# First pair's loads and rotation regrouped, and a new hand-placed order of the attention steps

## The chip, the cores and the metric

The kernel runs on one NeuronCore of a Trainium2 chip. The metric is the device time of one execution in microseconds (us). The engines are named as in the profile: PE is TensorE (matrix products and transposes), PEld its weight loads, DVE is VectorE, ACT is ScalarE, POOL is GpSimd, and SP is SyncE, whose queue (SPq) issues nearly all transfers.

## What is computed

The reference takes q, k and v of shape (2 batches, 8 heads, 576 positions, 64 columns), rotates q and k by the rotary tables, and computes softmax attention. Its output, 1152 tokens of 512 columns, goes through an RMS norm and a gated MLP (width 1536), and then through four expert MLPs whose outputs are weighted by the normalised domain probabilities. All is float32.

```python
def rotate(x):
    x1, x2 = (x[..., :half], x[..., half:])
    return np.concatenate([x1 * cos - x2 * sin, x1 * sin + x2 * cos], axis=-1)
q_rot, k_rot = (rotate(q), rotate(k))
scores = scale * np.matmul(q_rot, k_rot.transpose(0, 1, 3, 2))
attn = np.exp(scores - np.max(scores, axis=-1, keepdims=True))
attn = attn / (np.sum(attn, axis=-1, keepdims=True) + 1e-09)
return np.matmul(attn, v).astype(np.float32)
```

## The kernel before

Attention goes over eight pairs of heads (four pairs for each batch), `attention_pair` at L1096. Of a head's 576 positions the first 512 are "main": partition p holds positions 4p to 4p+3, so that a pair's main part is eight columns of 64 (j = 0 to 3 for the first head, 4 to 7 for the second). The last 64 positions of both heads share a ninth column, j = 8, the "left" rows. `rotate` (L551) does four steps with the tables -sin, sin and cos: two products into a scratch tile, a product in place, and a sum that lands in `turned`, tile by tile of 128 positions. `turn` (L604) transposes ten 64x64 pieces on PE into PSUM, copies the result into KQ (q scaled), and `dup` (L623) copies KQ's halves to the other partitions (KQ2) with two transfers on SP, since a head's scores need its keys and queries on both halves. For q such a copy has 144 KB, for k 72 KB.

For each pair there are nine tiles of scores, `s_step` (L650): matrix products into two PSUM banks, the row maximum on DVE (L680), the exponential on ACT (L684). `t_tile` transposes the exponentials and copies them to PTX; `pv` multiplies them with v; `scale` turns the reciprocal sums. Pair 0's first two tiles use own halves only and write both heads with one group (L664). When batch 0 is through, `rms_mean` (DVE, then twelve tiny operations on POOL from L848 on) and `rms_spread` prepare the norm.

Beside attention the first weights are prepared. SP loads 512 KB into a raw buffer (`w_load`, L363); ACT and DVE join and split it (`w_first`, `w_low`, `w_join`, `w_parts`), and `w_rest` (L470) subtracts on POOL (L472) or DVE. That frees the raw buffer, and `w_rest` at once puts the next load into SP's queue, where it waits for the subtraction. `free_raws` gives new raw buffers and loads into them.

The order of all these steps is written out by hand. Every step is entered with `at` (L217) in a fixed sequence; the table PLACE gives each entry its place in the sorted order, PICK its engine ("a", "v", "p"), BANK its PSUM bank, where a "." leaves the default. A step that takes PSUM banks through `ps_at` (L198) first issues the steps that still have to empty them. Each engine, and SP's queue, runs its instructions in the order in which they are issued, each after what it depends on. `keep_warm` (L585) issues transposes of the identity that only keep PE busy; "fill" steps are such groups.

Pair 0 differs: its loads, L1162 to L1169, are issued ahead of all, k and q by halves (one head of 512 positions each) and the tables in two parts of two transfers each on ACT's queue; its rotations are six entries, L1178 to L1183.

Of the kernel before, what the change touches and what calls it, by code (L numbers as in the profile page):

```python
# [128 lines left out]
]  # L129
PICK = (  # L130
    "............v..v..............................a.a.v.a.a.v.a.a.aaa...............vap....pvvppvpp.a..a"
    "..............................a.a.a.v.a.a.a.a.vaa...............vapv....pvpppppp.v..v..............."
    "...............a.a.v.a.v.v.a.v.aav...............avpp....pppppppp.v..a.............................."
    "a.a.a.a.a.a.a.a.aaa...............aapv....ppppvppp.v..a..............................v.a.a.v.a.a.a.v"
    ".ava...............aap....ppvpvppp.a..a..............................a.a.a.v.a.a.a.a.avv............"
    "...aavv....pvpppppp.a..a..............................v.a.a.a.a.a.a.a.ava...............avvp....pppp"
    "pppp.v..a..............................v.a.a.v.v.a.v.a.vvv...............avvp....p...p..p..p..p....."
    "............................p.p.p.v.p.p.p.v....v....v....v....v....a....v....v....a...p...p..p..p..v"
    "......"
)  # L140
BANK = (
    "......444446..4..............................6.4.4.6.4.6.4.4.4...6.....7.......4...............6..6."
    ".............................4.4.4.4.4.4.4.4.4...7.....7.......4................6..6................"
    "..............4.4.4.4.4.4.4.6.4...6.....6.......4................6..6..............................6"
    ".4.4.4.4.4.4.4.4...6.....6.......4................6..4..............................4.4.4.4.4.4.4.4."
# [9 lines left out]
def attention_moe_kernel(ctx, tc, q, k, v, w_gate, w_val, w_out, rms_g, probs, w1, w2, rope, out):  # L155
# [13 lines left out]
    nc = tc.nc  # L169
    B, H, S, D = q.shape  # L170
    P = 128
# [76 lines left out]
    def when(name):  # L248
        return lookup(name, POS, POS0, POS1, POSL)
# [1120 lines left out]
```

After attention come the gate and value products, then the expert products, whose code the change leaves alone.

## Time and profile before

| | us |
|---|---|
| median of three runs | 778.5 |
| lowest, highest | 778.1, 779.03 |
| the profiled execution | 778.99 |
| its span, first to last instruction | 777.0 |
| PE busy in the span | 751.6 |

The span is what the profile covers; the rest of the execution lies around it. PE's share is high in all, so the time depends on where PE has gaps, and on its granted clock, which the profile gives as a share of full speed: 1.00 is 2.4 GHz and 0.50 is 1.2 GHz.

### The profile page before, as it was taken

What the parts mean: (1) busy time and instruction counts of PE and PEld (TensorE: products, weight loads), DVE (VectorE), ACT (ScalarE), POOL (GpSimd) and SP (SyncE); (2) the same over time, 40 slices, a digit from 0 to 9 for tenths busy, and PEclk for the clock granted to TensorE, in tenths of its full rate; (3) what the DMA queues carried; (4) which work ended last, traced back from release to release, by engine and by line L of the source; (5) the groups of instructions that cost most, each with busy time, mean ns of one, the idle gap of its engine ahead of it and who ended that gap; (6) DMA issues with size and microseconds to landing.
All of it is one profiled execution on the core that took longest, in us unless ns stands there. A gap on an engine that the chain in (4) does not pass through costs nothing.

```text
span 777.0 us, 14117 instructions
## 1 busy us (share of the span) xinstructions
PE 751.6 (97%) x5590; PEld 661.9 (85%) x5590; DVE 454.5 (58%) x805; ACT 343.7 (44%) x635; POOL 391.9 (50%) x327
## 2 busy tenths in 40 slices
PE   7899987999999999999999999999999999999998
PEld 6556554768999899999999898988989899898996
DVE  6676786566588786676675445444444445444442
ACT  2777976653456344135444243332433424143330
POOL 6464847204556375137545655555464545546440
PEclk9999998999999999999999999999999999999999
DMA  4235333310113142214100110102102020110002
GB/s 123 72 105 148 90 121 86 108 56 1 56 55 103 61 139 79 82 35 156 55 28 28 55 55 28 56 27 64 45 28 82 1 82 28 54 56 0 1 28 95
DMA packets 43473, 50.00 MB, mean 64 GB/s; under 512 B 7184, under 2 KB 35600, under 8 KB 43408
## 3 DMA queue, kind: packets, MB, share of 16 engines
q1 hardware_dynamic: 42576, 48.66, 20.6%
q8 instruction: 44, 0.72, 0.4%
q10 hardware_dynamic: 832, 0.44, 0.2%
q14 instruction: 21, 0.17, 0.1%
HBM read 43.19 MB, written 2.36 MB: 59 GB/s over the span
## 4 chain that ended last, share of the span: by engine, by line
PE 80%; DVE 6%; issue 5%; POOL 4%; ACT 3%; DMA 2%; SPq 1%; ACTq 0%; POOLq 0%; DVEq 0%
PE PS L1024 26%; PE PS L1082 25%; PE PS L895 9%; PE PS L963 7%; PE PS L746 5%; PE PS L674 4%; PE PS L702 2%; POOL WS L472 1%; POOL WS L485 1%; POOL HB L1068 1%; PE PS L789 1%; DMA KQ<-KQ 1%; DVE nm L680 1%; ACT PTX L596 1%; ACT PP L684 1%
## 5 line engine op out<-in xcount | busy, mean ns | idle before, releaser
L1082 PE MATMUL PS<-WL,HB 128*128 128x512 f32 x675 | 165.0, 390 | 0.0
L1082 PEld LDWEIGHTS PS<-WL,HB 128*128 128x128 f32 x675 | 126.4, 188 | 27.1
L1024 PE MATMUL PS<-XT,WS 128*128 128x288 f32 x960 | 140.3, 295 | 0.2 <-DVE PP L1036 0.2
L1056 POOL TENSOR_TENSOR HB<-PP,HB 128x1152 fp32r<-128x1152 f32 x32 | 85.9, 2685 | 101.1 <-ACT PP L1055 100.7
L1024 PEld LDWEIGHTS PS<-XT,WS 128*128 128x128 f32 x960 | 131.6, 188 | 0.4 <-DVE PP L1036 0.4
L1024 PE MATMUL PS<-XN,WS 128*128 128x288 f32 x720 | 108.7, 295 | 1.5 <-ACT PP L1030 1.5
L895 PE MATMUL PS<-XN,WS 128*128 128x288 f32 (+1 forms) x672 | 104.5, 314 | 1.0 <-ACT GV L260 0.7
L895 PEld LDWEIGHTS PS<-XN,WS 128*128 128x128 f32 x672 | 101.1, 188 | 3.2 <-ACT GV L260 1.0
L1024 PEld LDWEIGHTS PS<-XN,WS 128*128 128x128 f32 x720 | 100.1, 188 | 2.7 <-ACT PP L1030 2.0
L1090 DVE SCALAR_TENSOR_TENSOR X<-PS,pr,X 128x512 f32<-128x512 f32 x63 | 46.7, 749 | 67.7 <-PE PS L1082 67.7
L1054 ACT ACTIVATE HB<-PP 128x1152 fp32r<-128x1152 f32 x32 | 37.3, 1167 | 106.1 <-DVE PP L1038 106.1
L963 PE MATMUL PS<-HB,WL 128*128 128x288 f32 (+1 forms) x528 | 76.6, 305 | 0.6 <-ACT X L969 0.6
L963 PEld LDWEIGHTS PS<-HB,WL 128*128 128x128 f32 x528 | 76.1, 188 | 0.8 <-ACT X L969 0.8
L680 DVE TENSOR_REDUCE nm<-PS 128x1 f32<-128x576 f32 x72 | 53.8, 754 | 27.7 <-PE PS L674 22.2
L485 POOL TENSOR_TENSOR WS<-RAW,WS 128x512 fp32r<-128x512 f32 (+1 forms) x40 | 47.9, 1215 | 34.9 <-ACT WS L484 28.5
L1031 DVE TENSOR_TENSOR PP<-PS,PP 128x288 f32<-128x288 f32 x40 | 18.3, 458 | 79.8 <-ACT PP L1030 71.7
L684 ACT ACTIVATE PP<-PS,nm 128x576 f32<-128x576 f32 x72 | 53.1, 740 | 24.7 <-DVE nm L680 24.4
L674 PE MATMUL PS<-KQ 64*128 64x288 f32 (+1 forms) x304 | 53.5, 453 | 9.3 <-ACT PP L684 4.6
L485 POOL TENSOR_TENSOR WS<-AR,WS 128x512 fp32r<-128x512 f32 (+1 forms) x40 | 46.6, 1181 | 21.2 <-ACT WS L484 18.5
L1082 PE MATMUL PS<-WS,HB 128*128 128x512 f32 x189 | 54.0, 394 | 0.0
L746 PE MATMUL PS<-PTX,VN 128*64 128x288 f32 x320 | 47.4, 420 | 0.1
L596 ACT ACTIVATE PTX<-PS 128x512 f32<-128x512 f32 (+4 forms) x63 | 36.1, 577 | 25.6 <-PE PS L702 23.6
(137 smaller groups left out, 1036.6 us busy)
## 6 DMA issues: line engine op xcount, KB each, us to landing
RAW<-in_moe_w_dram SPq DMA_DIRECT2D x16, 512.0 KB, 3.6
AR<-in_moe_w_dram SPq DMA_DIRECT2D x16, 512.0 KB, 3.6
RAW<-in_moe_w_gate_dram SPq DMA_DIRECT2D x10, 512.0 KB, 3.6
RAW<-in_moe_w_val_dram SPq DMA_DIRECT2D x6, 512.0 KB, 3.9
RAW<-in_moe_w_out_dram SPq DMA_DIRECT2D x6, 512.0 KB, 3.6
AR<-in_moe_w_out_dram SPq DMA_DIRECT2D x6, 512.0 KB, 4.5
AR<-in_moe_w_val_dram SPq DMA_DIRECT2D x6, 512.0 KB, 4.8
KQ<-KQ SPq DMA_DIRECT2D x16, 144.0 KB, 2.9
```

Of the source, the lines that this page charges most:

```text
L485: eng.tensor_sub(dst(1), src, f32(dst(0)))
L596: nc.scalar.activation(dst, src, AF.Copy, scale=1.0 if scale is None else scale)
L674: nc.tensor.matmul(box[0][rows, n, 0:HS], lhsT=queries(pair, i, c, n == i), rhs=keys(pair, i, n, n == i), start=True, stop=True,)
L680: nc.vector.tensor_reduce(nm[:, buf, j : j + 1], box[0][:, :, 0:HS], axis=AX.XY, op=ALU.max, negate=True)
L684: nc.scalar.activation(pp(pair, t)[:, o : o + S].rearrange("p (n t) -> p n t", n=2), box[0][:, :, 0:HS], AF.Exp, bias=nm[:, buf, j : j + 1 ...
L746: nc.tensor.matmul(box[0][HALF[h], :], lhsT=VN[:, pair % 2, 5 * h + k, :], rhs=PT[pair % 2][:, 4 if k == 4 else 5 * h + k, cols], start=(k ...
L895: nc.tensor.matmul(ps[:, 0:n], lhsT=w[:, lw, d, :], rhs=XN[:, lx, d, tok], start=(i == 0), stop=(i == 3 * ND - 1))
L963: nc.tensor.matmul(ps[:, 0:n], lhsT=w[:, lw, d * P : (d + 1) * P], rhs=hb(f, lx, tok), start=(i == 0), stop=(i == 11))
L1024: nc.tensor.matmul(ps, lhsT=w[:, lw, a, k, :], rhs=xs(b, lx, k, c), start=(i == 0), stop=(i == 5))
L1056: nc.gpsimd.tensor_sub(lo, q, f32(hi))
L1082: nc.tensor.matmul(ps, lhsT=hb(f, lx, slice(t * P, (t + 1) * P)), rhs=w[:, lw, :], start=(i == 0), stop=(i == 11),)
L1090: nc.vector.scalar_tensor_tensor(OA[:, t, :], in0=ps, scalar=p, in1=OA[:, t, :], op0=ALU.mult, op1=ALU.add)
```

## The change

Pair 0's k and q are loaded with one transfer each for both heads' main parts (plus the left rows as before), in the order k, left k, q, left q; the tables come in two transfers, both sine tables (288 KB) and the cosine table (144 KB). `rotate` takes a step `by`, so that columns 0 and 4, the first 128 queries of both heads, can be rotated alone; `turn_first` transposes them into KQ ahead of the other queries. k's main part is rotated in four operations in place of eight. The first warm-up has 54 in place of 60 pairs of transposes. All of PLACE, PICK and BANK is replaced. Among the places in the sorted order (806 steps before, 807 after) are these:

| step | before | after |
|---|---|---|
| rotations of pair 0: k columns 0-7; k left | 1, 2; 4 | 1; 2 |
| q: first 128 queries; other columns | 9; 5, 10 | 4; 7, 13 |
| pair 0, first tile's scores | 14 | 16 |
| pair 0, transposes of q (ten pieces) | 11 | 17 |
| loads of probabilities and g | 56 | 402 |
| first two weight loads | 288 | 318 |
| pair 4: copy of k; first scores | 302; 322 | 330; 331 |
| weight steps `w_rest` 0 and 1 | 374, 425 | 415, 420 |
| `w_first` 2 | 396 | 417 |
| pair 5: copies of k, q; first scores | 394, 404; 416 | 421, 425; 428 |
| `w_rest` 4; RMS chain on POOL | 512; 502 | 543; 520 |
| pair 6: copy of q; first scores | 532; 538 | 518; 528 |
| `w_rest` 6; third raw buffer; `w_rest` 7 | 596; 604; 697 | 680; 747; 748 |
| `w_first` 8 | 761 | 733 |

With the new banks, the second of the two first fillers writes the PSUM banks of k's transposes, so it comes after their copy.

```diff
--- before.py
+++ after.py
 PLACE = [
-    0, 8, 1, 3, 4, 9, 2, 6, 14, 22, 29, 5, 7, 20, 10, 12, 30, 23, 13, 28, 25, 21, 40, 42, 24, 43, 52, 31, 49, 61, 38,
...
+    0, 1, 3, 6, 12, 7, 9, 4, 10, 5, 19, 25, 2, 11, 26, 16, 36, 32, 57, 15, 20, 21, 18, 23, 34, 24, 38, 47, 31, 53, 45,
...
 ]
 PICK = (
-    "............v..v..............................a.a.v.a.a.v.a.a.aaa...............vap....pvvppvpp.a..a"
...
+    ".ppvv.a......v..a..............................a.a.a.v.a.a.a.a.ava...............vap....ppppvvvp.v.."
...
 )
 BANK = (
-    "......444446..4..............................6.4.4.6.4.6.4.4.4...6.....7.......4...............6..6."
...
+    ".....6.446446..4..............................4.4.4.4.6.6.4.4.4...7.....7.......4...............6..4"
...
 )
@@ -548,12 +548,12 @@
         for h in range(2) if last else ():
             queue.dma_start(out=dst[64 * h : 64 * h + 64, 8, :], in_=hs[h, MAIN:S, :])
 
-    def rotate(m, eng, j0=0, j1=9, tmp=tmp, steps=(0, 1, 2, 3)):
+    def rotate(m, eng, j0=0, j1=9, tmp=tmp, steps=(0, 1, 2, 3), by=1):
         x = (kn, qn)[m]
         eng = pick(eng)
-        nsin, sin, cos = (t[:, j0:j1] for t in tab)
-        x = x[:, j0:j1]
-        t = tmp.rearrange("p (j d) -> p j d", j=9)[:, j0:j1]
+        nsin, sin, cos = (t[:, j0:j1:by] for t in tab)
+        x = x[:, j0:j1:by]
+        t = tmp.rearrange("p (j d) -> p j d", j=9)[:, j0:j1:by]
         x4 = x.rearrange("p j (h d) -> p j h d", h=2)
         for step in steps:
             if step == 0:
@@ -561,16 +561,24 @@
             elif step == 1:
                 eng.tensor_mul(t[:, :, 32:64], x[:, :, 0:32], sin)
             elif step == 2:
-                eng.tensor_mul(x4, x4, cos.unsqueeze(2).to_broadcast([P, j1 - j0, 2, 32]))
+                eng.tensor_mul(x4, x4, cos.unsqueeze(2).to_broadcast([P, x.shape[1], 2, 32]))
+            elif by > 1:
+                eng.tensor_add(turned[m][:, 0:P].rearrange("p (h d) -> p h d", h=2), x, t)
             else:
                 for a, b in ((j0, min(j1, 8)), (8, j1)):
                     if a >= b:
                         continue
-                    dst = turned[m][:, MAIN:S].rearrange("p (h t d) -> p h t d", h=1, t=1)
-                    if b <= 8:
-                        dst = turned[m][:, 0:MAIN].rearrange("p (t h d) -> p h t d", t=4, h=2)[:, a // 4 : b // 4]
-                    i, o = ((y[:, a - j0 : b - j0].rearrange("p (h t) d -> p h t d", h=dst.shape[1])) for y in (x, t))
-                    eng.tensor_add(dst, i, o)
+                    dst = turned[m][:, MAIN:S].rearrange("p (j d) -> p j d", d=D)
+                    if b <= 8 and (a, b) != (0, 8):
+                        h = a // 4
+                        tiles = turned[m][:, 0:MAIN].rearrange("p (t h d) -> p h t d", t=4, h=2)
+                        dst = tiles[:, h, a - 4 * h : b - 4 * h]
+                    elif b <= 8:
+                        dst = turned[m][:, 0:MAIN].rearrange("p (t h d) -> p h t d", t=4, h=2)
+                        y, z = (w[:, a - j0 : b - j0].rearrange("p (h t) d -> p h t d", h=2) for w in (x, t))
+                        eng.tensor_add(dst, y, z)
+                        continue
+                    eng.tensor_add(dst, x[:, a - j0 : b - j0], t[:, a - j0 : b - j0])
 
     def load_v(pair):
         b, hp = divmod(pair, NPAIR)
@@ -631,6 +639,21 @@
         at(time, mm)
         later.append(at(time + when("kq_evac"), out))
         at(time + when("dup"), dup)
+
+    def turn_first(time):
+        box, later = [], []
+
+        def mm():
+            box.append(ps_at(6, 2, later))
+            for r in range(2):
+                nc.tensor.transpose(box[0][:, r, 0:64], turned[1][HALF[r], 0:P], ident[HALF[r], HALF[r]])
+
+        def out():
+            dst = KQ[:, 0, 1, 64:192].rearrange("p (r s) -> p r s", r=2)
+            evac(nc.vector, dst, box[0][:, :, 0:64], SCALE)
+
+        at(time, mm)
+        later.append(at(time + 0.1, out))
 
     def keys(pair, h, n, own):
         if own:
@@ -1106,7 +1129,7 @@
                 at(t0 + when(f"rot_k{i}"), rotate, 0, engine(f"rot_k{i}"), 0, 9, tmp, (i,))
                 at(t0 + when(f"rot_q{i}"), rotate, 1, engine(f"rot_q{i}"), 0, 9, tmp, (i,))
         turn(t0 + when("kT"), pair, 0, eng["kT"], slot("s_kT"))
-        turn(t0 + when("qT"), pair, 1, eng["qT"], slot("s_qT"))
+        turn(t0 + when("qT") if pair else 0.3, pair, 1, eng["qT"], slot("s_qT"))
         at(t0 + when("load_v"), load_v, pair)
         for t in range(5):
             both = [[]] if pair == 0 and t < 2 else None
@@ -1147,25 +1170,11 @@
 
         rope3 = rope.rearrange("p (a f) -> p a f", a=3)
 
-        def load_tab(j0, j1):
-            cols = slice(32 * j0, 32 * j1)
-            nc.scalar.dma_start(
-                out=TAB[0].rearrange("p (a f) -> p a f", a=2)[:, :, cols], in_=rope3[:, 0:2, cols]
-            )
-            nc.scalar.dma_start(out=TAB[1][:, cols], in_=rope3[:, 2, cols])
-
-        def load_head(dst, src, h, queue=nc.sync):
-            queue.dma_start(
-                out=dst[:, 4 * h : 4 * h + 4, :], in_=src[0, h, 0:MAIN, :].rearrange("(p t) d -> p t d", t=4)
-            )
-
-        load_head(kn, k, 0)
-        load_tab(0, 4)
-        load_head(qn, q, 0)
-        load_head(kn, k, 1)
-        load_tab(4, 9)
+        load_nat(kn, k, 0, False)
+        nc.scalar.dma_start(out=TAB[0].rearrange("p (a f) -> p a f", a=2), in_=rope3[:, 0:2, :])
+        nc.scalar.dma_start(out=TAB[1], in_=rope3[:, 2, :])
         load_nat(kn, k, 0, True)
-        load_head(qn, q, 1)
+        load_nat(qn, q, 0, False)
         load_nat(qn, q, 0, True)
         make_identity(nc, ident)
         nc.vector.memset(ones, 1.0)
@@ -1173,14 +1182,14 @@
             nc.gpsimd.memset(VN[HALF[1 - h], :, 5 * h + 4, :], 0.0)
         for x in turned:
             nc.vector.memset(x[:, S:640], 0.0)
-        keep_warm(60)
-
-        at(-20, rotate, 0, nc.vector, 0, 4, tmp)
-        at(-20, rotate, 1, nc.gpsimd, 0, 4, sq)
-        at(-19, rotate, 0, nc.vector, 4, 8, tmp)
-        at(-18, rotate, 0, nc.vector, 8, 9, tmp)
-        at(-17, rotate, 1, nc.vector, 4, 8, sq)
-        at(-17, rotate, 1, nc.gpsimd, 8, 9, sq)
+        keep_warm(54)
+
+        at(-20, rotate, 0, nc.vector, 0, 8, tmp)
+        at(-15.9, rotate, 0, nc.gpsimd, 8, 9, tmp)
+        at(-15.8, rotate, 1, nc.gpsimd, 0, 5, sq, (0, 1, 2, 3), 4)
+        at(-1.2, rotate, 1, nc.vector, 1, 4, sq)
+        at(-1.19, rotate, 1, nc.gpsimd, 5, 9, sq)
+        turn_first(-2)
 
         for i, time in enumerate(POS["fill"]):
             at(time, keep_warm, 8, int(i < 2))
```

## Rows read from the trace of the kernel before

**Rows 1.** The page: busy time, share of the span and instructions of each engine.
```profile
PE 751.6 (97%) x5590; PEld 661.9 (85%) x5590; DVE 454.5 (58%) x805; ACT 343.7 (44%) x635; POOL 391.9 (50%) x327
```

**Rows 2.** Stages: start:end, us, busy per engine (instructions), granted clock, DMA share, GB/s.
```profile
0.00:190.00 190.00, 170.84 (x1986) 118.83 (x1987) 125.99 (x231) 119.39 (x266) 92.49 (x123) 0.97 0.33 93
...
300.00:777.00 477.00, 473.11 (x2851) 436.70 (x2849) 240.75 (x443) 168.00 (x255) 236.22 (x156) 1.00 0.16 50
```

**Rows 3.** Timeline around 118 us: start, us, engine, line, operation, [idle before <-releaser].
```profile
113.25 0.20 POOL L848 TENSOR_TENSOR st<-st 128x5 f32<-128x5 f32 x1 [8.02 <-DVE st L841]
...
116.66 1.30 POOL L472 TENSOR_TENSOR WS<-RAW,WS 128x512 fp32r<-128x512 f32 x1
...
117.99 0.37 SPq L363 DMA_DIRECT2D RAW<-in_moe_w_gate_dram  x1
...
118.98 0.59 SPq L629 DMA_DIRECT2D KQ<-KQ  x1
...
124.40 0.84 PE L674 MATMUL PS<-KQ 64*128 64x288 f32 x1 [3.54 <-DMA KQ<-KQ]
```

**Rows 4.** Stretches where PE's granted clock fell, columns as in rows 2.
```profile
20.00:25.00 5.00, 4.80 (x50) 3.47 (x48) 3.07 (x5) 4.01 (x10) 2.75 (x3) 0.66 0.41 89
...
123.00:124.00 1.00, 0.00 (x0) 0.00 (x0) 0.00 (x0) 0.00 (x0) 1.00 (x3) 0.50 0.61 82
124.00:125.00 1.00, 0.60 (x4) 0.49 (x5) 0.00 (x0) 0.00 (x0) 0.81 (x1) 0.50 0.60 205
...
129.00:130.00 1.00, 1.00 (x18) 1.00 (x16) 0.51 (x1) 0.00 (x0) 0.15 (x1) 0.63 0.00 0
```

**Rows 5.** Timeline of the start, all engines, columns as in rows 3.
```profile
3.45 0.29 DVE L560 TENSOR_TENSOR AR<-AR,X 128x128 f32<-128x128 f32 x1 [2.40 <-DMA X<-rope_dram]
...
7.36 0.42 DVE L573 TENSOR_TENSOR AR<-AR,AR 128x256 f32<-128x256 f32 x1
...
8.67 0.67 PE L589 MATMUL PS<-ident 64*128 64x64 f32 x16
...
8.98 0.50 POOL L562 TENSOR_TENSOR AR<-AR,X 128x32 f32<-128x32 f32 x1
9.40 0.43 DVE L573 TENSOR_TENSOR AR<-AR,AR 128x256 f32<-128x256 f32 x1
...
9.75 0.82 DVE L598 COPY KQ<-PS 128x640 f32<-128x640 f32 x1
...
11.66 1.24 PE L664 MATMUL PS<-KQ 64*128 64x288 f32 x8 [0.92 <-DVE KQ L600]
...
12.93 1.42 DVE L680 TENSOR_REDUCE nm<-PS 128x1 f32<-128x576 f32 x2 [0.47 <-PE PS L664]
...
13.72 0.74 ACT L684 ACTIVATE PP<-PS,nm 128x576 f32<-128x576 f32 x1 [9.68 <-DVE nm L680]
...
15.72 1.08 POOL L562 TENSOR_TENSOR AR<-AR,X 128x288 f32<-128x288 f32 x1
...
16.83 0.76 DVE L564 TENSOR_TENSOR AR<-AR,X 128x576 f32<-128x576 f32 x1 [0.70 <-POOL AR L562]
...
17.51 1.42 DVE L680 TENSOR_REDUCE nm<-PS 128x1 f32<-128x576 f32 x2
...
19.02 0.69 ACT L596 ACTIVATE KQ<-PS 128x640 f32<-128x640 f32 x1
```

**Rows 6.** DMA in 0 to 40 us: GB/s in each of 40 slices.
```profile
GB/s 0 27 268 276 224 195 59 1 12 221 74 245 68 118 140 145 137 166 9 26 122 166 8 18 133 21 127 220 125 147 29 64 208 2 0 0 0 0 20 131
```

**Rows 7.** DMA issues (count, KB, us to landing) at 0, 64, 85 and 117 us.
```profile
AR<-in_k_dram SPq DMA_DIRECT2D x3, 256.0 KB, 2.8
...
KQ<-KQ SPq DMA_DIRECT2D x2, 144.0 KB, 2.4
...
RAW<-in_moe_w_gate_dram SPq DMA_DIRECT2D x1, 512.0 KB, 3.6
KQ<-KQ SPq DMA_DIRECT2D x2, 144.0 KB, 4.5
...
KQ<-KQ SPq DMA_DIRECT2D x2, 144.0 KB, 6.0
```

More of the change, by code (lines that the diff above doesn't have):

```diff
@@ L93 @@
 PLACE = [
[35 rows of a table removed]
[35 rows of a table added]
 ]
 PICK = (
-    "............v..v..............................a.a.v.a.a.v.a.a.aaa...............vap....pvvppvpp.a..a"
[L132 to L139, printed above, removed]
+    ".ppvv.a......v..a..............................a.a.a.v.a.a.a.a.ava...............vap....ppppvvvp.v.."
+    "a..............................a.a.v.a.a.a.v.a.avv...............avpp....pppvpvpp.v..a.............."
@@ new lines @@
+    "................a.a.v.a.a.a.a.a.vva...............avpv....pppppppp.v..a............................."
+    ".a.a.a.a.a.a.v.a.vav...............aapp....vvpppppv.v..a..............................a.a.a.a.a.a.a."
+    "a.aaa...............aap....pppppppp.v..a..............................v.a.a.v.a.a.a.a.vav..........."
+    "....avpv....pvpvpppp.a..a..............................a.a.a.v.v.a.a.v.aaa...............aapp....ppp"
+    "ppppp.v..a..............................a.a.a.a.a.v.v.a.aav...............aavv....p...p..p..v..p...."
@@ L140 @@
+    ".............................p.p.p.p.p.p.p.p....v....a....v....v....v....a....a....a...p...v..v..v.."
+    "p......"
 )
 BANK = (
-    "......444446..4..............................6.4.4.6.4.6.4.4.4...6.....7.......4...............6..6."
-    ".............................4.4.4.4.4.4.4.4.4...7.....7.......4................6..6................"
-    "..............4.4.4.4.4.4.4.6.4...6.....6.......4................6..6..............................6"
-    ".4.4.4.4.4.4.4.4...6.....6.......4................6..4..............................4.4.4.4.4.4.4.4."
@@ L146 @@
-    "4...6.....7.......4...............6..6..............................4.4.4.4.4.4.4.4.4...6.....6....."
-    "..4................6..6..............................4.4.4.4.4.4.4.4.4...7.....7.......4............"
-    "....6..6..............................4.6.4.4.4.4.4.4.6...6.....5.......4......4..6...............7."
-    ".5..7..7..5..7..7..7..6..5.................4....6....6..............................6..6............"
-    "......"
+    ".....6.446446..4..............................4.4.4.4.6.6.4.4.4...7.....7.......4...............6..4"
@@ new lines @@
+    "..............................4.4.4.4.4.6.4.4.4...6.....7.......4................6..6..............."
+    "...............4.4.4.4.4.4.6.6.4...6.....6.......4................6..6.............................."
+    "6.4.4.4.4.4.4.4.4...6.....6.......4................6..4..............................4.4.4.4.4.4.4.4"
+    ".4...6.....7.......4...............6..6..............................4.4.4.4.4.4.4.4.4...6.....6...."
+    "...4................6..6..............................4.4.4.4.4.4.4.4.4...7.....7.......4..........."
@@ L151 @@
+    ".....6..6..............................4.6.4.4.4.4.4.4.6...5.....6.......4......6..6...............7"
+    "..7..7..7..5..7..7..4..5..5.................6....6....6..............................6..6..........."
+    "......."
 )
```

68 rows, old and new, of the table PLACE are left out of this document.

## The prediction

> **What bounds the kernel now.** I read the profile from coarse to fine. The busy shares say that TensorE (PE) carries 751.6 of the 777.0 us [rows 1]; what a change of order and of start-up can win lies in the other 25.4 us, and in stretches where PE's clock was half. The stages show where these are: from 300 us on PE misses 3.9 us of 477, but in the attention part, 0 to 190 us, 19.2 us, at a mean granted clock of 0.97 [rows 2]; 2.3 are left for what lies between. All edits lie in that part, so I looked for its largest holes.
>
> The largest is at the start of pair 6. Its first scores wait 3.54 us for a copy of the rotated q inside SBUF, whose second half SP issued only at 118.98, right behind a weight load at 117.99 [rows 3]. The load waited for the buffer that POOL's L472 (116.66, 1.30 long) frees, and that stood in POOL's queue behind the chain of tiny RMS operations from 113.25 on, itself released by VectorE (DVE) after 8.02 us of idling. So one in-order chain (DVE, POOL, SP) held back a copy with which it has nothing to do. PE's clock then fell to 0.50 and stayed there until 129.6: of the stretch from 124.4 on, some 5.2 us of busy PE ran at half speed, 2.6 us of loss [rows 4]. Together 6.1 us.
>
> The second is the start. DVE's first rotation begins at 3.45, the first scores at 11.66, their maxima at 12.93, the first exponential at 13.72. The second tile's maxima begin only at 17.51, since DVE was held at 16.83 by a rotation of pair 1 that waited for POOL [rows 5]. Between 20 and 25 us the clock is 0.66, 1.7 us of loss if PE was the limit there [rows 4].
>
> **The start, step by step (-2.5 us).** Six transfers of k, q and tables become four; the left rows stay. Before its first operation DVE now needs all of k's main part and both sine tables, 544 KiB or 557 kB, where before 256 KiB sufficed. By the rate of each microsecond, 27, 268, 276, 224 GB/s [rows 6], 557 kB are there at 3.9 if nothing is mixed in, and at 4.75 with cosine and k's left rows; I take 4.5. The Trainium skill, "DMA: Bandwidth & Descriptors", section "Anatomy of one DMA", gives 2.0 us plus bytes over 436 GB/s for its path, which would put this at 4.0 and the sum at 7.0 instead of 6.5 us; the rates in these rows are lower, and I go by them.
>
> k's rotation is four DVE operations of 256, 256, 512 and 512 columns in place of eight that took 3.7 us together (3.45 to 7.36). With 0.43 for 256 columns and 0.76 for 576 four come to 2.4 at least, 3.7 at most if POOL disturbs them; I take 2.6: 7.1. k's left column goes to POOL, four operations of 0.50 or less, done near 6.5 beside DVE; POOL then rotates the first 128 queries, four more of about that size, by 8.5. PE's transposes take 0.04 each (16 in 0.67), ten of them 0.4 to 0.5, DVE's copy of them 0.82 [rows 5]: 8.6. The second filler now writes the banks of that copy and so waits for it, 0.67 more, then the two early transposes and their copy on ACT: first scores about 9.9 instead of 11.66. DVE still has to rotate the other q columns, 1.1 and 1.6 us by the 0.29 and 0.43 of its operations on 128 and 256 columns, until 11.4; so maxima at 11.4 instead of 12.93. ACT empties the late q transposes first (0.69 [rows 5]): first exponential about 12.7 instead of 13.72, 1.0 earlier. The second tile gains more: pair 1's k can be loaded from 7.1 on and lands 2.8 later [rows 7], POOL's two products of 1.08 end near 12.3, DVE's maxima (1.42 for two) at 12.8 and its two steps of 0.76 at 14.4 [rows 5], so the second maxima come at 14.5 instead of 17.51, 3.0 earlier. I take 2.5, nearer to that row because all later tiles hang on it; ends 0 and 3.5. Twelve fewer warm-up transposes cost nothing: PE waits for k's rotation there, and without that wait they would be 0.6 us won.
>
> **Moved steps.** By the new list pair 6's copy of q stands ten steps before pair 6's first scores and 25 before the weight step whose load blocked it; the RMS chain stands after it too. The 3.54 us and the clock loss of 2.6 go: -6.1, ends 0 and -6.1. What is late next is pair 6's own q transposes: seven groups of PE work between them and the scores cover the copy, 0.
>
> The other side is pair 5. There the weight steps 0 and 1 stand directly ahead of both copies, so SP issues two 512 KB loads and a q load just before them. A 144 KB copy landed 2.4 us after its issue with nothing large ahead, 4.5 behind a 256 KB load, 6.0 behind a weight load [rows 7]. I price the new wait at 4.5 - 2.4 = 2.1 us, by the middle row, because SP can run ahead of PE there; ends 0 (PE has twelve groups between the q transposes and the scores) and 6.1 (as pair 6 now). At pair 4 the first two loads also move ahead of the k copy, but twelve PE groups after k's transposes are emptied cover it: 0, or again 2.1 without them.
>
> The five small loads of probabilities move from pair 1 to pair 4, behind copies instead of ahead: 0, as SP is not the limit in pair 1. The third raw buffer is given 143 steps later, and weight loads 8 and 9 with it; their first use is 53 steps on: 0, or up to 2.3 us if the middle part's idling doubles. Engines and banks of many copies change too; idle time in the other attention stretches may go either way by 1 us, taken as 0.
>
> **Sum.** -2.5 - 6.1 + 2.1 = -6.5 us. The profiled execution took 778.99, 2.0 around its span of 777.0, and lies 0.5 above the median 778.5; against itself the sum gives 772.5, against the median 772.0.
>
> **Rivals.** (a) Better: the first clock fall goes as well. For it: its stretch follows PE's idling that the late second maxima made. Against: the first pair stays thin. 772.0 - 1.7 = 770.3; with pair 5 free of waits 768.2. (b) The stall moves whole from pair 6 to pair 5, clock fall included: -2.5 - 6.1 + 6.1, 776.0. For it: same queue, twice the bytes. Against: POOL can free these buffers early. (c) As (b), and the earlier start is lost again in pair 1, whose q load now waits until 11.4 for the last q rotation: 778.5, no change. (d) Slower: ACT's first step on weight load 2 now stands two steps behind the one that frees its buffer, where it stood 22 behind. If POOL reaches that less than 1.3 + 3.6 us [rows 3, 7] ahead of ACT, ACT waits for the load, and pair 4's last exponentials behind it. Its price is up to 4.9 us of PE and 2.6 of clock, and the copy behind the same load adds 3.5 instead of 2.1: -2.5 - 6.1 + 7.5 + 3.5 = +2.4, 780.9. For it: the in-order chain of pair 6 is the same. Against: POOL has little else queued there. (e) That the change does nothing is excluded by the list of steps.
>
> **How the numbers follow.** Forecast 0.45, (a) 0.13, (b) 0.17, (c) 0.10, (d) 0.15. A measurement here tells 0.2%, 1.6 us, from none. Faster: 0.45 + 0.13 + 0.17 = 0.75; same 0.10; slower 0.15. Low end: start -3.5, clock -1.7, pair 6 -6.1, no wait at pair 5: -11.3, 767.2. The high end takes in (c): 778.6. The forecast's own range is 769.5 to 774.5.
>
> **What would show it.** Right: first scores near 9.9, second maxima near 14.5, no half clock near 125 us and no wait for the KQ copy at pair 6; a KQ wait of 1 to 3 us at pair 5. Wrong: ACT idle for a weight load in pair 4, a wait of over 3 us on a copy followed by a half clock, or first scores later than 11 us. From 300 us on nothing should differ.

## The result and the profile after

The changed kernel takes 766.55 us (median of four runs, 766.08 to 767.41) where the kernel before took 778.67 in the same comparison (four runs): ratio 0.9846, interval 0.9829 to 0.9863. It is 12.1 us faster. The forecast was 772.0, with a range down to 767.2, so the direction was right and the size was about half of what came; the measured time lies just below the range.

The page of the kernel after, its first part [rows 1], and the stages [rows 2]:

```profile
PE 746.3 (97%) x5580; PEld 657.7 (86%) x5580; DVE 451.2 (59%) x800; ACT 345.9 (45%) x641; POOL 388.1 (51%) x324
```

```profile
0.00:190.00 190.00, 177.15 (x2062) 126.13 (x2063) 130.37 (x240) 126.88 (x283) 93.97 (x125) 0.99 0.34 93
300.00:765.60 465.60, 461.54 (x2784) 425.08 (x2782) 233.97 (x429) 163.60 (x247) 229.30 (x149) 1.00 0.15 49
```

From 300 us on PE misses 4.1 us, as before (3.9). In the attention part it misses 12.9 instead of 19.2, at a mean clock of 0.99 instead of 0.97. So what the change won of PE's idle time lies there.

The start of the kernel after, all engines, columns as in [rows 5]:

```profile
5.19 0.42 DVE L560 TENSOR_TENSOR AR<-AR,X 128x256 f32<-128x256 f32 x1 [4.14 <-DMA AR<-in_k_dram]
...
6.71 0.69 DVE L579 TENSOR_TENSOR AR<-AR,AR 128x512 f32<-128x512 f32 x1
...
11.13 1.24 PE L687 MATMUL PS<-KQ 64*128 64x288 f32 x8 [0.30 <-DVE KQ L608]
11.16 1.28 ACT L604 ACT_TABLE_LOAD   x1 [11.16 <-DVE KQ L608]
...
12.41 1.42 DVE L703 TENSOR_REDUCE nm<-PS 128x1 f32<-128x576 f32 x2
...
12.89 0.70 ACT L604 ACTIVATE KQ<-PS 128x640 f32<-128x640 f32 x1 [0.44 <-PE PS L625]
...
13.49 0.74 ACT L707 ACTIVATE PP<-PS,nm 128x576 f32<-128x576 f32 x1
...
15.96 1.42 DVE L703 TENSOR_REDUCE nm<-PS 128x1 f32<-128x576 f32 x2
```

DVE's first rotation begins at 5.19 instead of 3.45; its four operations end at 7.40, where the eight ended at 7.78 [rows 5]. First scores come at 11.13 (before 11.66), first maxima at 12.41 (12.93), the first exponential at 13.49 (13.72): little. The second tile's maxima come at 15.96 instead of 17.51: there the start gains 1.55 us.

Pairs 5 and 6, SP's queue and what hangs on it, timeline around 86 and 110 us; compare [rows 3]:

```profile
86.17 0.37 SPq L363 DMA_DIRECT2D RAW<-in_moe_w_val_dram  x1
...
89.16 0.54 SPq L636 DMA_DIRECT2D KQ<-KQ  x1
...
89.75 0.59 SPq L637 DMA_DIRECT2D KQ<-KQ  x1
...
92.56 1.19 PE L697 MATMUL PS<-KQ 64*128 64x288 f32 x8
```

```profile
107.21 0.20 POOL L871 TENSOR_TENSOR st<-st 128x5 f32<-128x5 f32 x1
...
109.78 0.60 SPq L637 DMA_DIRECT2D KQ<-KQ  x1
...
112.03 1.30 POOL L472 TENSOR_TENSOR WS<-RAW,WS 128x512 fp32r<-128x512 f32 x1 [1.35 <-ACT WS L465]
113.36 0.39 SPq L363 DMA_DIRECT2D RAW<-in_moe_w_gate_dram  x1
...
114.35 1.02 PE L697 MATMUL PS<-KQ 64*128 64x288 f32 x4
```

At pair 6 both halves of q's copy are issued by 109.78, ahead of the weight load at 113.36, and the scores at 114.35 have no wait: the step went as forecast. At pair 5 the two weight loads stand ahead of the copies, as the list of steps said, but the scores at 92.56 do not wait either (idle time before an instruction would stand in brackets behind it): the forecast wait of 2.1 us did not come.

Stretches of PE's clock in the kernel after, columns as in [rows 2]; compare [rows 4]:

```profile
20.00:25.00 5.00, 4.64 (x68) 2.94 (x69) 3.82 (x6) 4.67 (x13) 0.15 (x1) 1.00 0.47 107
110.00:115.00 5.00, 4.27 (x27) 2.65 (x27) 4.17 (x8) 3.54 (x9) 2.55 (x5) 0.66 0.35 72
```

The first fall is gone. The second has moved from 123 to 130 us to 111 to 115 us, and is shorter. Summed over windows of 1 us up to 200 us, PE's idle time falls from 19.2 to 12.9 us, and what its half clock costs (busy time times the share missing) from 4.3 to 1.7: 8.9 of the 11.4 us between the two spans. The rest is busy time at full clock; 12 transposes fewer are some 0.5 of it, and what makes up the others the rows don't say.

### The profile page after: what moved, and what is told of

It reads as the page before. It is cut to its first block, busy times and chain, and to the rows that moved or that the text cites. A ratio compares the mean times of both kernels' runs of the same rounds, so it can differ in the third digit from the quotient of the medians.

```text
span 765.6 us, 14083 instructions
## 1 busy us (share of the span) xinstructions
PE 746.3 (97%) x5580; PEld 657.7 (86%) x5580; DVE 451.2 (59%) x800; ACT 345.9 (45%) x641; POOL 388.1 (51%) x324
## 4 chain that ended last, share of the span: by engine, by line
PE 80%; DVE 6%; issue 5%; POOL 4%; ACT 3%; DMA 1%; SPq 0%; POOLq 0%; DVEq 0%; ACTq 0%
PE PS L1047 27%; PE PS L1105 26%; PE PS L918 8%; PE PS L986 7%; PE PS L769 5%; PE PS L697 4%; PE PS L725 2%; ACT PP L707 1%; POOL WS L485 1%; PE PS L812 1%; DMA AR<-in_k_dram 1%; POOL WS L472 1%; DVE nm L703 1%; POOL HB L1091 1%; DVE RAW L409 1%
## 5 line engine op out<-in xcount | busy, mean ns | idle before, releaser
L697 PE MATMUL PS<-KQ 64*128 64x288 f32 (+1 forms) x304 | 50.1, 442 | 3.6 <-ACT PP L707 3.3
L604 ACT ACTIVATE PTX<-PS 128x512 f32<-128x512 f32 (+4 forms) x66 | 38.4, 589 | 11.6 <-PE PS L725 6.4
```

Source lines behind the costliest of these rows:

```text
L604: nc.scalar.activation(dst, src, AF.Copy, scale=1.0 if scale is None else scale)
L697: nc.tensor.matmul(box[0][rows, n, 0:HS], lhsT=queries(pair, i, c, n == i), rhs=keys(pair, i, n, n == i), start=True, stop=True,)
```

## The experiments

Each table of places, engines and banks can be cut: the steps up to a number in the order of one kernel, all others in the order of the other. A changed place is one line behind the tables, so line numbers of such kernels are one to three higher.

| run | median us | ratio to before (interval) |
|---|---|---|
| kernel after | 766.55 | 0.9846 (0.9829-0.9863) |
| before, copy of pair 6 earlier (b_copy) | 774.57 | 0.9956 (0.9944-0.9968) |
| before, two maxima earlier (b_max) | 778.21 | 1.0009 (0.9999-1.0019) |
| new start, 20 steps (h_start) | 780.31 | 1.0027 (1.0015-1.0038) |
| new start, 130 steps (h_s130) | 780.30 | 1.0026 (1.0016-1.0035) |
| the same, small loads later (h_s130b) | 774.56 | 0.9953 (0.9941-0.9966) |
| the same, and the copy earlier (h_s130c) | 770.58 | 0.9897 (0.9882-0.9912) |
| old start, 22 steps (h_rest) | 769.18 | 0.9884 (0.9867-0.9900) |
| old start, 132 steps (h_r130) | 770.72 | 0.9909 (0.9892-0.9927) |
| old order to step 430 (h_late) | 770.95 | 0.9908 (0.9895-0.9922) |
| new order to step 545 (h_a545) | 769.58 | 0.9893 (0.9875-0.9912) |
| old order and copy to step 545 (h_c545) | 775.18 | 0.9966 (0.9953-0.9980) |
| after, pair 5's v loads earlier (a_vload) | 771.63 | 0.9912 (0.9900-0.9925) |
| after, a product emptied earlier (a_pvout) | 767.01 | 0.9860 (0.9842-0.9878) |
| that, an ACT step later (a_parts) | 766.91 | 0.9856 (0.9842-0.9870) |
| that, RMS spread later (a_best) | 769.65 | 0.9891 (0.9873-0.9909) |

The kernel before took 778.0 to 778.1 us (medians) beside them. The kernel after was timed only in the first comparison, where before took 778.67, so a difference between a run and the kernel after is uncertain by some 0.6 us more than its interval says.

**The copy of pair 6 alone.**

```diff
+PLACE[524] = 509.5
```

> Kernel before, with one place changed: pair 6's copy of q is issued right after pair 6's q transposes are emptied, ahead of the RMS chain and of the weight load that stood before it in SP's queue. Theory A (the pair 6 stall is one removable term): the 3.54 us wait for the KQ copy is gone; with the half clock behind it (2.6 us) also gone the time falls by 5 to 6 us against before, by 3.5 if the clock falls all the same. Theory B (the wait covered another one, which takes its place: DVE's chain or ACT's exponentials are late at the same point): PE waits there for another releaser, and the time falls by under 2 us.

Timeline of this kernel around 115 us, and PE's windows there:

```profile
114.80 0.46 SPq L629 DMA_DIRECT2D KQ<-KQ  x1
...
115.31 0.61 SPq L630 DMA_DIRECT2D KQ<-KQ  x1
...
117.49 0.37 SPq L364 DMA_DIRECT2D RAW<-in_moe_w_gate_dram  x1
...
120.43 0.75 PE L675 MATMUL PS<-KQ 64*128 64x288 f32 x4
```

```profile
115.00:116.00 1.00, 0.23 (x8) 0.09 (x4) 0.94 (x3) 1.00 (x2) 0.68 (x4) 1.00 0.08 18
116.00:117.00 1.00, 0.75 (x4) 0.35 (x4) 0.96 (x2) 1.00 (x5) 0.99 (x2) 0.73 1.02 226
117.00:118.00 1.00, 1.00 (x10) 0.30 (x8) 0.66 (x2) 0.40 (x1) 1.00 (x2) 0.50 0.25 51
```

3.5 us faster. One place, and the scores find their copy. That this equals the wait of 3.54 is chance. Between 90 and 150 us PE's idle time falls by only 2.5 us (8.3 to 5.9, below), because behind the place of the old wait two new ones for DVE stand, 1.01 us at 123.52 and 0.36 at 124.59, which the kernel before does not have. The other 1.0 us is half clock (2.7 to 1.6): the clock falls all the same, only earlier, behind the waits for exponentials that were there before. So the 2.6 us of half clock in the forecast did not hang on this wait alone.

**The start.** First the second tile's maxima alone:

```diff
+PLACE[25] = 33.3
+PLACE[28] = 33.4
```

> Kernel before, with two places changed: in pair 0 the maxima of the second tile stand on DVE ahead of the step of pair 1's q rotation that waited for POOL. The loads and the rotation of pair 0 stay as before. Theory A (the first clock fall hangs on PE's gap while the second tile's maxima are late): second maxima near 16.8 instead of 17.51, first clock fall shorter or gone, 0.7 to 2.4 us faster than before. Theory B (it is the thin work of the first pair altogether, and the fall goes only with the whole new start): clock of 0.66 between 20 and 25 us as before, gain of 0 to 0.7 us.

No difference: theory A's trace with theory B's time. In the profiled run the second maxima came at 16.31 and the clock was 1.00 between 20 and 25 us, yet the median is that of the kernel before. In that profile PE idled 8.7 us up to 60 us, where before it idled 7.9, so part of the 1.7 came back as waiting. One stretch in one profile was a poor witness for what this fall costs on average.

Then the new start alone, with 20 steps (the cut is shown against the kernel after):

```diff
 PLACE = [
-    0, 1, 3, 6, 12, 7, 9, 4, 10, 5, 19, 25, 2, 11, 26, 16, 36, 32, 57, 15, 20, 21, 18, 23, 34, 24, 38, 47, 31, 53, 45,
+    0, 1, 3, 6, 12, 7, 9, 4, 10, 5, 19, 30, 2, 11, 23, 16, 20, 31, 24, 15, 29, 26, 18, 41, 43, 25, 44, 53, 32, 50, 62,
...
```

> The new start alone: the loads, rotations and first 20 steps of the kernel after, then the order, engines and banks of the kernel before. Theory A (start and first clock fall are one term, kept to the end): first scores near 11.1, clock of 1.00 between 20 and 25 us, 3 to 4 us faster than before, and the KQ wait of pair 6 is there as before. Theory B (the earlier start is mostly used up by later tiles in the old order, and the fall stays): 0.5 to 1.5 us faster, clock near 0.66 between 20 and 25 us.

Neither: 2.2 us slower. Timeline of this kernel, 10 to 17 us:

```profile
12.48 0.82 DVE L608 TENSOR_SCALAR KQ<-PS 128x640 f32<-128x640 f32 x1 [0.42 <-PE PS L625]
...
13.22 1.41 DVE L703 TENSOR_REDUCE nm<-PS 128x1 f32<-128x576 f32 x2
...
14.05 1.28 ACT L707 ACT_TABLE_LOAD   x1 [14.05 <-DVE nm L703]
...
15.35 0.74 ACT L707 ACTIVATE PP<-PS,nm 128x576 f32<-128x576 f32 x1
...
16.23 2.53 PE L687 MATMUL PS<-KQ 64*128 64x288 f32 x7 [2.16 <-ACT PP L707]
```

The cut had given the copy of q's transposes back to DVE, ahead of the maxima, so these ended late; and ACT's first instruction was the exponential, behind whose maxima its table load of 1.28 us stood in full. In the kernel after, ACT empties q's transposes, and the load, at 11.16, is over before these are there. The trace puts the loss on these two, the engine of one copy and the place of the table load; no run changes either alone.

With 130 steps both stand as in the kernel after:

> The loads and rotations of the kernel after and its first 130 steps (all of pair 0 and the beginning of pair 1), then the order, engines and banks of the kernel before. In the run with 20 steps the copy of pair 0's q transposes had fallen to DVE ahead of the first maxima, and ACT's table load came only after these; here both stand as in the kernel after. Theory A (the start is one term, worth what the two traces show at equal PE work up to 75 us, and it lasts): clock 1.00 between 15 and 25 us, the KQ wait of pair 6 as before, 3.5 to 4.5 us faster than before. Theory B (the start's gain is used up at the join or at pair 6, where DVE's and POOL's chain is late anyway): 0 to 2 us faster.

Again 2.3 us slower, but by another wait, at the join of the two orders:

```profile
38.54 0.19 DVE L1164 TENSOR_REDUCE GV<-pr 128x9 f32<-128x36 f32 x1 [5.20 <-DMA pr<-in_moe_domain_probs_dram]
...
39.34 0.82 DVE L608 TENSOR_SCALAR KQ<-PS 128x640 f32<-128x640 f32 x1
...
40.21 1.23 PE L769 MATMUL PS<-PTX,VN 128*64 128x288 f32 x4 [5.35 <-DVE KQ L608]
```

DVE stood for 5.20 us before the normalisation of the probabilities, whose four loads of at most 8 KB SP issued only from 33.94 on. DVE's copy at 39.34 stood behind it in the queue, and PE waited 5.35 us for that copy. At equal PE work the kernel had been 4.2 us ahead up to there. So the loads and the normalisation were put further back:

```diff
+PLACE[678] = 146.5
+PLACE[679] = 248.5
```

> As the run with the new start and 130 steps, but the small loads of the probabilities stand behind pair 2's copies and their normalisation at pair 3's first scores, so that DVE does not wait 5.2 us for them at the join of the two orders. Theory A (the start is one term of 3.5 to 4.5 us that lasts, and the join alone had hidden it): no wait of PE over 1.5 us before pair 6, the KQ wait or half clock at pair 6 as before, 3.5 to 4.5 us faster than the kernel before. Theory B (it is used up behind the join in any case): 0 to 2 us faster.

3.5 us faster, theory A: the start is a term of its own and lasts. Its clock is 1.00 from 15 to 25 us, and at pair 6 PE waits 2.5 us for the KQ copy with 0.50 behind it, as before. That the early fall goes with the new start is borne out by the profiles of all runs here: of the seven with the old start six have a fall within the first 25 us, and of the nine with the new start and at least 130 steps eight have none up to 60 us; the ninth is the run above, whose clock fell at 37 us in its wait of 5.35. With the copy's place added:

```diff
+PLACE[525] = 510.5
```

> The run before this one, and pair 6's copy of q issued ahead of the RMS chain as in the run with that place alone. Theory A (the two terms add): 3.5 to 4.5 plus 3.5, so 7 to 8 us faster than the kernel before, some 4 to 5 us short of the kernel after, which then come from the order of pairs 4 to 6. Theory B (the start and the copy are the whole gain, since the clock then holds at pair 6 as well): 10 to 12 us faster.

7.5 us faster: the two terms add, and 4.0 us to the kernel after are left.

**The new order without the new start.** Old loads and 22 old steps, then the new order:

> The new order without the new start: loads, rotations and first 22 steps of the kernel before, then the order, engines and banks of the kernel after. Theory A (the parts add up): 12.1 less the 3 to 4 us of the start, so 8 to 9 us faster than before. Theory B (the first fall of the clock goes by the order of the steps after the first 22, not by the loads): 10 to 11 us faster, with a clock of 1.00 between 20 and 25 us.

8.9 us: theory A; the fall had moved to 10 to 15 us (0.66). With 132 old steps:

> Loads, rotations, engines, banks and the first 132 steps of the kernel before, then the order, engines and banks of the kernel after; the counterpart of the run with the new start and 130 steps. Theory A (parts add): 12.1 less the 3.5 to 4.5 us of the start, so 7.5 to 8.5 us faster than before, clock 0.66 between 20 and 25 us, no KQ wait in pairs 5 and 6. Theory B (the new order needs the early start to keep its copies covered): a KQ wait of 1 us or more appears in pair 5 or 6, and the gain is under 6 us.

7.3 us, no KQ wait, and the fall again at 11 to 15 us: theory A, 0.2 us below its range. With the first 430 steps old:

> Loads, rotations, engines, banks and the first 430 steps of the kernel before (up to the beginning of pair 5's scores), then the order, engines and banks of the kernel after. Theory A (what is left of the gain beside the start sits in the order from pair 5 on): 7 to 8 us faster than before, as the run with the old start and 132 steps, no KQ wait at pair 6. Theory B (the order of pairs 1 to 4 carries part of it): 3.5 to 5.5 us faster.

7.2 us: theory A. So the steps from 132 to 430, most of pairs 1 to 4, carry nothing that can be measured, and the new order from pair 5 on is worth 3.6 us more than the copy alone. Where, the stretch from 90 to 150 us shows, columns as in [rows 2], in the kernel before, with the copy alone, and in this run:

```profile
90.00:150.00 60.00, 51.66 (x543) 34.63 (x540) 42.20 (x76) 41.12 (x89) 33.55 (x41) 0.94 0.39 114
```

```profile
90.00:150.00 60.00, 54.13 (x592) 36.40 (x591) 44.45 (x80) 44.26 (x97) 33.21 (x41) 0.97 0.39 114
```

```profile
90.00:150.00 60.00, 56.50 (x649) 38.95 (x646) 44.40 (x81) 47.47 (x106) 35.69 (x42) 1.00 0.40 114
```

PE misses 8.3, 5.9 and 3.5 us, at a mean clock of 0.94, 0.97 and 1.00. Between the last two lie 2.4 us of idle time, and by 1 us windows 1.6 of half clock: 4.0, near the 3.6 of the medians. The waits in this stretch (engine, line, waited for: us in all, times, longest), copy alone:

```profile
PE PS L747 <- DVE X L876: 1.0, 1, 1.0
PE PS L703 <- DVE GV L266: 0.9, 1, 0.9
PE PS L618 <- DVE RAW L411: 0.8, 1, 0.8
...
PE PS L790 <- DVE rr L773: 0.4, 1, 0.4
```

and with the new order from step 430 on:

```profile
PE PS L702 <- DVE RAW L410: 0.6, 1, 0.6
PE PS L746 <- DVE X L875: 0.5, 1, 0.5
PE PS L617 <- DVE KQ L598: 0.2, 1, 0.2
```

PE waits for DVE 3.1 and 1.3 us; for exponentials 2.2 and 1.9. So between these two runs the idle time that went is time in which PE waited for DVE (weight joins, the norm's scaling, copies). That the new order gains by serving DVE's queue better is argued from this, not shown, and two other profiles speak against it as a general account. In the same stretch the kernel before waits for DVE

```profile
PE PS L617 <- DVE RAW L410: 1.0, 1, 1.0
PE PS L702 <- DVE GV L265: 0.9, 1, 0.9
```

and the kernel after

```profile
PE PS L769 <- DVE X L781: 1.5, 1, 1.5
PE PS L725 <- DVE RAW L410: 0.9, 1, 0.9
PE PS L625 <- DVE KQ L606: 0.2, 1, 0.2
```

which is 1.9 and 2.6 us: in the kernel after more than before. Its idle time there is 4.6 us and its half clock 1.7. Two cuts at step 545 were to place this more closely:

> Loads, rotations, engines, banks and the first 545 steps of the kernel after (up to the second tile of pair 6), then the order, engines and banks of the kernel before. Theory A (the 3.5 to 4 us left over sit in pair 5 and the beginning of pair 6: fewer waits for exponentials and for DVE around the RMS norm): 10.5 to 12 us faster than before. Theory B (they sit in pairs 6 and 7 and the gate products): 7 to 8.5 us faster.

> The counterpart: loads, engines, banks and the first 545 steps of the kernel before, with pair 6's copy of q ahead of the RMS chain, then the order, engines and banks of the kernel after. Theory A (nothing from step 545 on): as the run with the copy alone, 3.5 to 4.5 us faster than before. Theory B: 7 to 8 us faster, with the 1.3 us of PE's idling between 135 and 150 us gone.

The second fits theory A: 2.8 us, no more than the copy alone (3.5). By this the 4.2 us between it and the run cut at 430 would sit in steps 430 to 545. Not all of them need to, for behind its join it has a wait that neither the kernel with the copy alone nor the run cut at 430 has at this length:

```profile
135.73 0.46 PE L702 MATMUL PS<-ident,PP 64*128 64x64 f32 x8 [1.79 <-DVE RAW L410]
```

The run cut at 430 waits 0.56 us for a weight join at 130.99. The first cut falls in theory B's range and far from A's: 8.4 us faster, 3.0 us above the kernel after by the medians, though up to 115 us it was as fast. Behind its join PE waited 3.4 us in five waits between 115 and 137 us, the longest 1.43 for a copy on DVE, where the kernel after waits 1.3. So each of the two runs has a loss at its own join, the two theories are not decided, and whether steps behind 545 add something of their own stays open.

**The wait that did not come.**

```diff
+PLACE[441] = 423.5
```

> Kernel after, with one place changed: the four loads of pair 5's v, some 2.2 us of issuing on SP, stand ahead of pair 5's copy of q instead of behind it. Theory A (the copy of q, issued until 90.3 us for scores at 92.56, has under 0.5 us to spare; the forecast wait at pair 5 failed only because the copies were issued in time): PE waits 1.5 to 2.5 us for the KQ copy at pair 5, and the time is 1.5 to 2.5 us above the kernel after, so some 10 us below before; more if the clock falls behind the wait. Theory B (the cover of twelve PE groups is wide enough for a late copy): no KQ wait, time as the kernel after, 12 us below before.

Timeline of this kernel at pair 5:

```profile
91.70 0.35 SPq L589 DMA_DIRECT2D VN<-in_v_dram  x1
...
93.93 0.55 SPq L637 DMA_DIRECT2D KQ<-KQ  x1
...
96.40 1.48 PE L698 MATMUL PS<-KQ 64*128 64x288 f32 x6 [3.06 <-DMA KQ<-KQ]
```

SP first waited until 91.70 for v's buffer, then issued, and the copy went out at 93.93 instead of 89.16. PE waited 3.06 us, and the clock was 0.79 and 0.87 in the next two stretches of 5 us, 1.7 us by 1 us windows: 4.8 together, and the time is 5.1 us above the kernel after. Theory A, and more, as the fall came too. The cover of this copy is thin; the kernel after only issues it in time.

**Taking out waits of the kernel after.** The longest is 1.49 us at 95.55, for pair 3's second product, which DVE empties behind the normalisation and a join:

```diff
+PLACE[331] = 416.5
```

> Kernel after, with one place changed: pair 3's second product with v is emptied on DVE ahead of the normalisation of the probabilities and of a weight join, for which PE waited 1.49 us at 95.55. Theory A (a removable wait on PE's path): the wait goes, 1.0 to 1.5 us faster than the kernel after, 13 to 13.6 us below before. Theory B (it only moves: the maxima or the join that now stand behind it on DVE are late by 0.5 us, and ACT's exponentials with them): within 0.5 us of the kernel after.

767.01, no difference that can be told. The wait was gone, but in the profile (of a run 2.8 us above the median) PE waited 1.72 us at 96.30 for an ACT copy, which stood behind ACT's own wait of 2.15 us for DVE's weight join. So that ACT step was moved too:

```diff
+PLACE[331] = 416.5
+PLACE[732] = 447.5
```

> Kernel after, with two places changed: pair 3's second product with v is emptied ahead of the normalisation, as in the run with that place alone, and ACT's last step on weight load 2, which there waited 2.15 us for DVE with two copies of exponentials behind it, stands behind pair 4's last copies. Theory A (that in-order wait on ACT is what the first wait moved to): neither wait is there, 1.0 to 2.0 us faster than the kernel after, 13 to 14 us below before. Theory B (PE's work then waits on the next thing, POOL's subtraction or the maxima, within two tiles): within 0.5 us of the kernel after.

766.91, theory B. Its four runs are 766.17 and 766.19 at a mean clock of 1.000, 767.63 and 768.27 at 0.998. Last, the RMS spread behind the copies as well:

```diff
+PLACE[683] = 527.5
```

> Kernel after with three places changed: the two of the run before it (pair 3's second product emptied earlier, ACT's last step on weight load 2 later), and the spread of the RMS norm behind the copies of pair 6, ahead of whose scores PE waited 0.8 us for POOL. Theory A (the three waits are PE's own, and the clock holds): 2 to 3 us faster than the kernel after, 14 to 15 us below before. Theory B (as in the two runs before, PE then waits for the next thing within two tiles): within 0.7 us of the kernel after.

769.65, 3.1 us slower than the kernel after; neither theory had that. PE's windows in this kernel:

```profile
110.00:115.00 5.00, 4.45 (x33) 2.78 (x35) 3.46 (x6) 3.16 (x8) 2.06 (x2) 0.67 0.45 134
115.00:120.00 5.00, 3.93 (x26) 2.32 (x26) 3.48 (x10) 2.78 (x6) 3.52 (x4) 0.50 0.36 105
120.00:125.00 5.00, 5.00 (x57) 3.79 (x54) 2.88 (x6) 3.45 (x9) 4.64 (x6) 0.80 0.13 41
```

Up to 200 us PE idles 12.1 us, less than in the kernel after (12.9), but the half clock costs 4.6 instead of 1.7. Still, the clock does not explain the 3.1 us: of its six runs one took 768.45 us at a mean clock of 1.000 and another 768.45 at 0.994. What made it slower stays open. No version tried beats the kernel after.

## Why the prediction was right and wrong

**Start, -2.5: measured -3.5 with the old order behind it and -4.8 with the new (12.1 less the 7.3 of the old start with 132 steps), for partly other reasons.** First scores were forecast at 9.9 and came at 11.13. The landing was taken at 4.5 and DVE began at 5.19. The copy of the first queries stood on DVE, behind part of a rotation, not on ACT. The second maxima came at 15.96 instead of the forecast 14.5. PE's idle time fell by only 1.3 us up to 30 us (6.4 to 5.1) and by 2.2 up to 60 us (7.9 to 5.7). The rest, as far as one profile of each kernel tells, is the first clock fall of 1.7, which is rival (a). The Trainium skill, "DMA: Bandwidth & Descriptors", section "Anatomy of one DMA", gives 2.0 us plus bytes over 436 GB/s for one transfer that GpSimd issues. The estimate of 4.0 for the landing carried this over to three transfers from SP's and ACT's queues; for these it does not hold here, since DVE began at 5.19.

**Pair 6, -6.1: measured -3.5 alone, -4.0 beside the new start.** The wait went as described, by the cause described. Two steps failed. The price of the wait was taken whole, but 1.4 us of new waits for DVE stood behind it, and the idle time fell by 2.5 us instead of 3.54. And all 2.6 us of the half clock were given to this wait: with it gone the clock fell earlier, behind waits for exponentials, and 1.0 us was saved; in the kernel after the fall costs 1.7 in the profiled run.

**Pair 5, +2.1: measured 0.** The queue was read rightly, and the price was of the right kind, as the run with v's loads ahead shows. The step that failed is that loads ahead of a copy delay it by their landing. They were issued at the latest at 86.17, 3.0 us ahead of q's copies, and these, issued at 89.16 and 89.75, landed 3.2 and 3.1 us later, where the price had taken 4.5. So the scores at 92.56 had no wait.

**Moved steps taken as 0: measured some -3.6.** This is the largest error. "Engines and banks of many copies change too ... taken as 0" stood for the whole new order from pair 5 on. Between the run with the copy alone and the run cut at 430 PE's idle time from 90 to 150 us fell by 2.4 us, of which 1.8 is waits for DVE, and the half clock of 1.6 went. That the order took the half clock away is not shown, since the profile with the old order to step 545 has none from 60 to 200 us either. Which of the moved steps did it stays open. The rows of before could have shown a part: the waits for DVE of 1.0 and 0.9 us, passed over for the one of 3.54. The two that stood behind that one could not be seen there.

The sum by the runs, -3.5 for the start and -7.2 from step 430 on, is -10.7 against -12.1 measured; the intervals of about 1 us each cover the difference.

**Rivals.** (a) came true, with pair 5 free of waits: 768.2 as worked out, 1.7 above the measured time, and 0.13 was too little for it. What the absent fall gives in time alone is not shown, as the run with two maxima earlier lost it in its profile and gained nothing. (b), (c) and (d) did not happen. Of (d) a small form was seen, ACT standing 2.15 us for DVE with a PE wait of 1.72 behind it, but only after a place was changed. That nothing differs from 300 us on was right.

## What to carry to other kernels

In a kernel whose order is written by hand, price the many waits of about 1 us, not only the longest one: here the order around them was worth 3.6 us, as much as taking out the one 3.5 us stall. A long wait also covers shorter ones behind it, which appear when it goes. A wait and the half clock behind it are two terms: the first goes with its cause, the second may only move to the next weak place. When a step moves past others in a queue, ask when these were issued and what they wait for, not just how many bytes stand ahead. And a kernel cut together from two orders has waits at its join that neither order has, so a loss behind the join says little of the parts.

## What the runs showed of the hardware

PE's clock falls differ between executions of one kernel. For the version with an ACT step later the four runs are 766.2 us twice at a mean clock of 1.000, and 767.6 and 768.3 at 0.998. But the mean clock does not order the times in general: the kernel after took 766.84 at 1.000 and 766.26 at 0.997, and the last version 768.45 at both 1.000 and 0.994. With the same steps up to 60 us the profile of the kernel before has 1.7 us of half clock there and that of the run cut at step 430 has 3.2, at an idle time of 7.9 and 7.8 us.

ACT's table load of 1.28 us stood at 2.76 in the kernel before, waiting for nothing, at 11.16 in the kernel after, behind the first copy on DVE, and at 14.05, on the path, with the new start and 20 steps; what decides this the runs don't show. And four loads of at most 8 KB held DVE for 5.20 us, and PE for 5.35, in the run with 130 steps: the instruction that needed them stood in DVE's queue from 33.34 on, and SP issued them from 33.94 on.
